# A gated linear attention with an MLP behind it: hand-woven streams against one-engine tasks in a list scheduler's order

## The chip, the core and the metric

The kernel runs on one core of a Trainium2 chip. The metric is the device time of one execution in microseconds (us), as the median of several. The core has five engines that run side by side, each through its own queue and strictly in the order of that queue: TensorE (PE, matrix products and transposes, results to PSUM alone), VectorE (DVE), ScalarE (ACT, exponentials, logs, silu, copies), GpSimd (POOL[...]) and SyncE (SP, which here only starts transfers). They meet through semaphores. So the order in which a kernel emits its instructions is part of its performance: an instruction that is not ready holds all those behind it on its engine.

## The reference: what is computed

Four batches, 8 heads, 768 time steps, head dimension 48. An attention with a forget gate, then an MLP with a silu over all 3072 tokens:

```python
f = 1.0 / (1.0 + np.exp(-f_logit))
for t in range(S):
    state = f[:, :, t, :, None] * state + einsum('bhd,bhe->bhde', k[:, :, t], v[:, :, t])
    y[:, :, t] = einsum('bhd,bhde->bhe', q[:, :, t], state)
x = y.transpose(0, 2, 1, 3).reshape(B * S, H * D)     # 3072 x 384
h = x @ w_in                                          # w_in: 384 x 2048
out = (h * sigmoid(h)) @ w_out                        # w_out: 2048 x 384
```

The kernel works in chunks of 128 time steps. A chunk of all four batches is a *group* g (0 to 5), two of its batches are a *half group*. Within a chunk the loop over time becomes matrix products: the gates' logs are summed along time (`cs`, a product with a triangle of ones), k is multiplied by exp of the sum (`ki`), q by exp of minus the sum (`qg`), both are transposed, their products are masked by the triangle (`atm`), and the output is the masked scores times v plus q times the state before the chunk. The state is then moved on by `d_ps` and the chunk's total decay (`al`).

## The kernel before

Nested Python generators emit the work. Each function below takes one piece of it; most contain steps of several engines in a row (cut to what matters):

```python
def logs(g, lo, hi):                       # ACT, a half or a whole group at once
    f = loaded[g, "f"][:, lo:hi]
    nc.scalar.activation(f, f, AF.Exp, scale=-1.0)
    nc.scalar.activation(lf[g % 3][:, lo:hi, :, 0:D], f, AF.Ln, bias=1.0)

def decays(g, b):                          # PE, then ACT twice
    cs = cps.tile([C, H, D], F32, name="cs", tag="cs")
    nc.tensor.matmul(cs, triu, lf[g % 3][:, b, :, 0:D], start=True, stop=True)
    ...
    nc.scalar.activation(ias[b], cs, AF.Exp, scale=1.0)
    ...
    nc.scalar.activation(aas[b], cs, AF.Exp, scale=-1.0)

def scale_k(g, b):                         # POOL
    nc.gpsimd.tensor_mul(ki[g % 2][:, b, :, 0:D], loaded[g, "k"][:, b], ias[b])
def scale_q(g, b):                         # DVE
    nc.vector.tensor_mul(qg[g % 2][:, b, :, 0:D], loaded[g, "q"][:, b], aas[b])
...
def attend(g, lo, hi):                     # the attention of the units (g, b)
    for s in range(len(units) + 3):
        if s < len(units):
            transposes(g, units[s]);       yield T_COST    # t_ps (PE), qk (DVE)
        if 1 <= s <= len(units):
            scores(g, units[s - 1]);       yield A_COST    # a_ps (PE), atm (DVE)
        if 2 <= s <= len(units) + 1:
            outputs(g, units[s - 2]);      yield Y_COST    # y_ps (PE), y (DVE)
            if g < NCH - 1:
                state(g, units[s - 2]);    yield D_COST    # d_ps (PE), st (DVE)
        if s >= 3:
            turn(g, units[s - 3]);         yield X_COST    # x_ps (PE), xT (DVE)
```

The MLP of a group, in two halves of its work ("in" and "out"):

```python
def mlp_in(g, lo, hi):
    w = (hi - lo) * C                      # 512 columns, or 256 for a half group
    per = MT // w
    for n in range(0, NT, per):
        h_ps = hps.tile([128, per, w], F32, name="h_ps", tag="h_ps")
        for j in range(per):
            for kk in range(KT):           # KT = 3
                nc.tensor.matmul(h_ps[:, j], w_in_sb[:, kk, ...], xT[g][:, kk, lo:hi]..., ...)
        nc.scalar.activation(hT[g][:, n:n + per, lo * C:hi * C], h_ps, AF.Silu)
        yield 650.0

def mlp_out(g, lo, hi):
    for b in range(lo, hi):
        o_ps = hps.tile([C, d_model], F32, name="o_ps", tag="h_ps")
        for n in range(NT):                # NT = 16, a yield after each 4
            nc.tensor.matmul(o_ps, hT[g][:, n, b * C:(b + 1) * C], w_out_sb[:, n, :], ...)
            ...
        nc.scalar.copy(o_sb, o_ps)
        nc.scalar.dma_start(out=out[r0:r0 + C, :], in_=o_sb)
```

PSUM has eight banks, shared out as follows: `cs`/`al_ps` one, `y_ps`/`d_ps`/`x_ps` ("yd") two, `t_ps` one, `a_ps` two, `h_ps`/`o_ps` two. The streams are merged by a rule of proportion (the one with the smallest share of its estimated cost emits next), with leads and splits set by hand:

```python
def interleave_gen(*streams):
    live = [[g, float(total), 0.0] for g, total in streams]
    while live:
        s = min(live, key=lambda s: s[2] / s[1])
        ...
for g in range(1, NCH):
    first = [(mlp_in(g, *span), mlp_cost(*span))]
    ...                                    # with the first 54% of attend(g + 1)
    run(*first)
    second = [(mlp_out(g, *span), mlp_cost(*span))]
    ...                                    # with the rest of attend(g + 1)
        exp_ln_tables()
        logs(g + 2, *ALL)
        lead = 4000.0 if g == 1 else 2000.0
        second.append((chain(wait(lead), prep(g + 2, *ALL, g > 1)), lead + prep_cost(*ALL)))
    run(*second)
```

Group 0 and the beginning of group 1 are written out by hand, with matrix products of zeros (`warm`) in between that keep TensorE's clock up. Inputs arrive by halves for groups 0 and 1 and as whole groups later; after group 0, a tiny transfer (`behind`) that reads a row of `w_out_sb` makes SyncE wait, so that the weights come ahead of group 1.

Of the kernel before, what the change touches and what calls it, by code (L numbers as in the profile page):

```python
# [10 lines left out]
F32 = mybir.dt.float32  # L11
# [6 lines left out]
def interleave_gen(*streams):  # L18


    live = [[g, float(total), 0.0] for g, total in streams]
    while live:
        s = min(live, key=lambda s: s[2] / s[1])
        try:
            s[2] += next(s[0])
            yield
        except StopIteration:
            live.remove(s)


def chain(*gens):
    for gen in gens:
        yield from gen


def once(fn, *args):
    fn(*args)
    yield 330.0
# [3 lines left out]
def kernel(  # L42
# [19 lines left out]
    MT = B * C  # L62

    singles = ctx.enter_context(tc.tile_pool(name="singles", bufs=1))
    ld = ctx.enter_context(tc.tile_pool(name="ld", bufs=2))
    wk = ctx.enter_context(tc.tile_pool(name="wk", bufs=2))
    gk = ctx.enter_context(tc.tile_pool(name="gk", bufs=2))
    hp = ctx.enter_context(tc.tile_pool(name="hp", bufs=2))
    op = ctx.enter_context(tc.tile_pool(name="op", bufs=3))
    cps = ctx.enter_context(tc.tile_pool(name="cps", bufs=1, space=PSUM))  # L70
# [3 lines left out]
    hps = ctx.enter_context(tc.tile_pool(name="hps", bufs=2, space=PSUM))  # L74
# [4 lines left out]
    def load(g, name, b0=0, b1=B):  # L79
        if (g, name) not in loaded:  # L80
            loaded[g, name] = ld.tile([C, B, H, D], F32, name=f"{name}_ld", tag=f"{name}_ld")
        t = loaded[g, name]
        src = SRC[name].rearrange("b h s d -> s (b h) d")[g * C:(g + 1) * C, b0 * H:b1 * H]
        nc.sync.dma_start(out=t[:, b0:b1].rearrange("p b h d -> p (b h) d"), in_=src)

    HB = B // 2
    FIRST, SECOND = (0, HB), (HB, B)
    ALL = (0, B)
    for span in (FIRST, SECOND):
        for name in "fkqv":  # L90
            load(0, name, *span)


    lf = [singles.tile([C, B, H, 64], BF16, name=f"lf{i}") for i in range(3)]
    qg = [singles.tile([C, B, H, 64], BF16, name=f"qg{i}") for i in range(2)]
    ki = [singles.tile([C, B, H, 64], BF16, name=f"ki{i}") for i in range(2)]
    vb = [singles.tile([C, B, H, D], BF16, name=f"vb{i}") for i in range(2)]
# [10 lines left out]
    def load_w_in():  # L108
        src = moe_w_in.rearrange("(ko ki) n -> ki ko n", ki=128)
        for n in range(0, d_ff, 512):  # L110
            nc.gpsimd.dma_start(out=w_in_sb[:, :, n:n + 512], in_=src[:, :, n:n + 512])  # L111
            yield

    def load_w_out():
        src = moe_w_out.rearrange("(ko ki) n -> ki ko n", ki=128)
        for n in range(0, NT, 4):
            nc.gpsimd.dma_start(out=w_out_sb[:, n:n + 4, :], in_=src[:, n:n + 4, :])
            yield

    def exp_ln_tables():  # L120
        nc.scalar.preload_act_table_set("natural_log_exp_and_others")

    alast = {}
    ias = {}
    aas = {}

    def logs(g, lo, hi):

        f = loaded[g, "f"][:, lo:hi]
        nc.scalar.activation(f, f, AF.Exp, scale=-1.0)  # L130
        nc.scalar.activation(lf[g % 3][:, lo:hi, :, 0:D], f, AF.Ln, bias=1.0)  # L131

    def decays(g, b):

        cs = cps.tile([C, H, D], F32, name="cs", tag="cs")
        nc.tensor.matmul(cs, triu, lf[g % 3][:, b, :, 0:D], start=True, stop=True)  # L136
        ias[b] = wk.tile([C, H, D], F32, name="ia", bufs=4)
        nc.scalar.activation(ias[b], cs, AF.Exp, scale=1.0)  # L138
        aas[b] = wk.tile([C, H, D], F32, name="a", bufs=4)
        nc.scalar.activation(aas[b], cs, AF.Exp, scale=-1.0)  # L140

    def scale_k(g, b):
        nc.gpsimd.tensor_mul(ki[g % 2][:, b, :, 0:D], loaded[g, "k"][:, b], ias[b])  # L143

    def scale_q(g, b):
        nc.vector.tensor_mul(qg[g % 2][:, b, :, 0:D], loaded[g, "q"][:, b], aas[b])  # L146

    def scale(g, b):
        scale_k(g, b)
        scale_q(g, b)  # L150
        values(g, b)

    def values(g, b, engine=None):
        src, dst = loaded[g, "v"][:, b], vb[g % 2][:, b]
        if engine is nc.scalar:
            nc.scalar.copy(dst, src)
        else:
            nc.gpsimd.tensor_copy(dst, src)  # L158

    def lasts(g, lo, hi):  # L160
        al_ps = cps.tile([C, B, NP], F32, name="al_ps", tag="cs")
        for b in range(lo, hi):
            for p in range(NP):
                nc.tensor.matmul(al_ps[:, b, p:p + 1], lf[g % 3][:, b, 2 * p:2 * p + 2, :], ones,
                                 start=True, stop=True)
        if g not in alast:
            alast[g] = gk.tile([C, B, NP], F32, name="al")
        nc.scalar.activation(alast[g][:, lo:hi], al_ps[:, lo:hi], AF.Exp, scale=-1.0)

    xT = {}  # L170
    qkT = {}
    atm = {}

    def transposes(g, b):
        i = g % 2
        t_ps = tps.tile([128, 2, NP, C], BF16, name="t_ps")
# [321 lines left out]
```

## Time and profile before

| what | before |
|---|---|
| median of 3 runs | 221.41 us (220.03 to 221.65) |
| profiled run | 220.49 us, span on the core 218.7 us |
| mean granted TensorE clock | 0.961 |
| in tiles: matmuls into h_ps | 192 of 256 columns, 284 ns each as recorded, and 192 of 512 columns, 379 ns |
| out chunks: matmuls into o_ps | 384 of 384 columns, 330 ns |
| silu, one tile of 128x512 | 96 at 597 ns |
| activation table loads | 12 at 1283 ns |
| copy of k scaled (GpSimd) / q scaled (VectorE) | 24 at 1035 ns / 24 at 1012 ns |
| masking of scores (VectorE) | 48 at 686 ns |
| traffic | 25.17 MB read, 4.72 MB written |

How to read it: the span is the time between the first and the last instruction. TensorE's matmuls are pipelined, so the recorded mean of one (330 ns) is longer than the distance between two, and a busy TensorE is not one at its peak. What a row of pieces in the chain of waits gives ("PE o_ps L293 x4", 0.65 us) is nearer to its price. Idle time of an engine that nobody waits for costs nothing; what counts is which wait ends last in a stretch. In the lists, L286 is a line of the kernel, the number before it is the start in us, and the next is how long it took.

### The profile page before, as it was taken

Reading aid. Unit: us, or ns where it says so; the run is one execution under the profiler, and the core shown is the slowest. Engines: PE = TensorE matmul, PEld = TensorE weight load, DVE = VectorE, ACT = ScalarE, POOL = GpSimd, SP = SyncE. Lnnn points to the kernel's source line nnn. Section 1 sums busy time; section 2 is a strip of 40 time slices with the busy share of each in tenths; the row PEclk is TensorE's granted clock in tenths of the full one; section 3 lists DMA queues with packets and bytes.
Section 4 is the critical chain, followed back from the end, with each engine's and each line's share of the span. In section 5 each row is a group of like instructions: output and inputs, shape, how many; then the busy total and the mean of one; then the engine's idle time right before and its main releaser. Section 6 shows DMA issues by size and latency. Waiting matters only on the chain.

```text
span 218.7 us, 4193 instructions
## 1 busy us (share of the span) xinstructions
PE 190.7 (87%) x1740; PEld 117.8 (54%) x1740; DVE 105.3 (48%) x189; ACT 126.2 (58%) x209; POOL 47.7 (22%) x66
## 2 busy tenths in 40 slices
PE   6485899976887687998899998999998999999993
PEld 3244478643675356865455655555654456643561
DVE  3258533126847068787755575456574455200000
ACT  3538267753566555686677846668647760167510
POOL 4317600032320281009200173000462000000000
PEclk9769589999999699999999999999999999999999
DMA  8998999999999999999999962000110000210011
GB/s 138 187 187 111 147 197 181 171 226 197 211 215 165 201 214 214 172 175 221 215 166 198 190 120 76 1 0 3 72 39 36 0 3 36 72 39 0 0 72 72
DMA packets 106034, 27.00 MB, mean 123 GB/s; under 512 B 99360, under 2 KB 106016, under 8 KB 106016
## 3 DMA queue, kind: packets, MB, share of 16 engines
q1 hardware_dynamic: 98848, 18.88, 59.9%
q0 software_dynamic: 3712, 3.15, 9.5%
q10 hardware_dynamic: 3456, 4.72, 6.6%
q8 instruction: 13, 0.21, 0.4%
q14 instruction: 5, 0.04, 0.1%
HBM read 25.17 MB, written 4.72 MB: 137 GB/s over the span
## 4 chain that ended last, share of the span: by engine, by line
PE 60%; DMA 11%; DVE 11%; ACT 9%; POOL 3%; issue 3%; SPq 1%; ACTq 1%; DVEq 0%
PE o_ps L293 22%; PE h_ps L283 22%; DMA w_out_sb<-in_moe_w_out_dram 6%; DVE qg L146 5%; PE t_ps L179 5%; PE a_ps L189 4%; DMA q_ld<-in_q_dram 3%; DMA f_ld<-in_f_logit_dram 2%; DVE qk L181 2%; DVE atm L193 2%; ACT o_sb L298 2%; PE y_ps L211 1%; POOL w_in_sb L111 1%; PE y_ps L215 1%; PE cs L136 1%
## 5 line engine op out<-in xcount | busy, mean ns | idle before, releaser
L283 PE MATMUL h_ps<-xT,w_in_sb 128*128 128x256 bf16 (+1 forms) x384 | 74.6, 332 | 3.7 <-DVE xT L202 1.4
L286 ACT ACTIVATE hT<-h_ps 128x512 bf16<-128x512 f32 x96 | 56.8, 597 | 30.5 <-PE h_ps L283 28.8
L293 PE MATMUL o_ps<-w_out_sb,hT 128*128 128x384 bf16 x384 | 73.0, 330 | 0.1
L283 PEld LDWEIGHTS <-w_in_sb 128*128 128x128 bf16 x384 | 35.1, 99 | 26.2 <-issue 6.0
L293 PEld LDWEIGHTS <-hT 128*128 128x128 bf16 x384 | 35.3, 98 | 25.8 <-issue 6.6
L143 POOL TENSOR_TENSOR ki<-k_ld,ia 128x384 bf16<-128x384 f32 x24 | 24.8, 1035 | 110.8 <-ACT ia L138 110.8
L193 DVE TENSOR_TENSOR atm<-a_ps,triu 128x512 bf16<-128x512 f32 x48 | 30.9, 686 | 17.5 <-PE a_ps L189 17.5
L146 DVE TENSOR_TENSOR qg<-q_ld,a 128x384 bf16<-128x384 f32 x24 | 23.7, 1012 | 21.1 <-ACT a L140 14.9
L298 ACT COPY o_sb<-o_ps 128x384 f32<-128x384 f32 x24 | 11.5, 477 | 25.4 <-PE o_ps L293 25.0
L181 DVE COPY qk<-t_ps 128x1024 bf16<-128x1024 bf16 x24 | 16.6, 690 | 17.7 <-PE t_ps L179 17.7
L241 DVE TENSOR_TENSOR st<-d_ps,al 48x192 bf16<-48x192 f32 x40 | 14.2, 354 | 17.6 <-PE d_ps L237 17.2
L138 ACT ACTIVATE ia<-cs 128x384 f32<-128x384 f32 x24 | 11.8, 490 | 17.7 <-PE cs L136 15.3
L158 POOL CAST vb<-v_ld 128x384 bf16<-128x384 f32 x22 | 15.3, 699 | 6.0 <-DMA v_ld<-in_v_dram 6.0
L130 ACT ACTIVATE f_ld<-f_ld 128x768 f32<-128x768 f32 (+1 forms) x8 | 9.3, 1163 | 11.0 <-DMA f_ld<-in_f_logit_dram 11.0
L136 PE MATMUL cs<-lf,triu 128*128 128x384 bf16 x24 | 8.2, 342 | 8.0 <-ACT lf L131 4.3
L179 PE MATMUL t_ps<-ident,qg 128*128 128x128 bf16 x96 | 9.8, 227 | 5.4 <-DVE qk L181 3.6
L202 DVE CAST y<-y_ps 128x384 bf16<-128x384 f32 x22 | 12.2, 553 | 4.2 <-PE y_ps L215 4.0
L179 PEld LDWEIGHTS <-qg 128*128 128x128 bf16 x96 | 7.5, 100 | 10.8 <-issue 5.4
L189 PE MATMUL a_ps<-qk 48*128 48x128 bf16 x192 | 10.2, 229 | 2.6 <-DVE atm L193 2.6
L189 PEld LDWEIGHTS <-qk 48*128 48x128 bf16 x192 | 5.8, 98 | 11.0 <-issue 7.2
L140 ACT ACTIVATE a<-cs 128x384 f32<-128x384 f32 x24 | 11.7, 486 | 0.0
L215 PE MATMUL y_ps<-vb,atm 128*128 128x48 bf16 x192 | 11.4, 185 | 0.0
(40 smaller groups left out, 145.7 us busy)
## 6 DMA issues: line engine op xcount, KB each, us to landing
out_dram<-o_sb ACTq DMA_DIRECT2D x24, 192.0 KB, 2.1
f_ld<-in_f_logit_dram SPq DMA_DIRECT2D x4, 768.0 KB, 10.3
k_ld<-in_k_dram SPq DMA_DIRECT2D x4, 768.0 KB, 11.1
q_ld<-in_q_dram SPq DMA_DIRECT2D x4, 768.0 KB, 11.1
v_ld<-in_v_dram SPq DMA_DIRECT2D x4, 768.0 KB, 11.4
f_ld<-in_f_logit_dram SPq DMA_DIRECT2D x4, 384.0 KB, 5.4
k_ld<-in_k_dram SPq DMA_DIRECT2D x4, 384.0 KB, 6.2
q_ld<-in_q_dram SPq DMA_DIRECT2D x4, 384.0 KB, 6.6
```

The lines of the kernel that those rows point to most:

```text
L143: nc.gpsimd.tensor_mul(ki[g % 2][:, b, :, 0:D], loaded[g, "k"][:, b], ias[b])
L146: nc.vector.tensor_mul(qg[g % 2][:, b, :, 0:D], loaded[g, "q"][:, b], aas[b])
L158: nc.gpsimd.tensor_copy(dst, src)
L179: nc.tensor.transpose(t_ps[:, j, p, :], src[i][:, b, 2 * p:2 * p + 2, :], ident)
L181: nc.vector.tensor_copy(sb, t_ps)
L189: nc.tensor.matmul(a_ps[:, r, p, :], qkT[b][lo:lo + D, 1, p, :], qkT[b][lo:lo + D, 0, p, :], start=True, stop=True)
L193: nc.vector.tensor_mul(sb[:, r], a_ps[:, r], triu[:, None, :].to_broadcast([C, NP, C]))
L241: nc.vector.tensor_mul(st[b][lo:lo + D, :, r * D:(r + 1) * D], d_ps[lo:lo + D, :, r * D:(r + 1) * D], alast[g][lo:lo + D, b, :, None].to_b ...
L283: nc.tensor.matmul(h_ps[:, j], w_in_sb[:, kk, (n + j) * 128:(n + j + 1) * 128], xT[g][:, kk, lo:hi].rearrange("p b c -> p (b c)"), start=( ...
L286: nc.scalar.activation(hT[g][:, n:n + per, lo * C:hi * C], h_ps, AF.Silu)
L293: nc.tensor.matmul(o_ps, hT[g][:, n, b * C:(b + 1) * C], w_out_sb[:, n, :], start=(n == 0), stop=(n == NT - 1))
L298: nc.scalar.copy(o_sb, o_ps)
```

## The change

The generators are gone. The work is described as tasks, each on one engine, with an estimated duration, the tasks it needs, the buffer that it takes and those it frees, the activation table it uses, and a rank. A list scheduler in Python runs over them while the kernel is being built, always taking the task that can start first (of several that can, on one engine, the one of lowest rank), and the instructions are emitted in the order of its start times. The MLP tasks have ranks above 1000, so on TensorE attention goes first and the MLP fills what is left. "In" and "out" tasks follow modes, so that ScalarE need not swap its tables at each silu; the filler of zeros is put into planned gaps until the first MLP task. What it is for: no engine's queue should have a task at its head that waits while one behind it is ready.

Beside the order, these things change:

- everything goes by half groups (12 of them): loads (four buffers of half groups in place of two of whole ones), logs, the MLP (always 256 columns, two blocks to a tile);
- `cs` and `al_ps` go into the two "yd" banks, and `h_ps`/`o_ps` get a third bank;
- `behind` reads row 4 of `w_out_sb` (second quarter of the weight) in place of row 10 (third quarter), and all weights are issued in one go;
- the copies out of PSUM that ScalarE made at the start (y and xT of the first units) are VectorE's.

The core of the diff (cut; the removed code is that above):

```diff
+class Plan:
+    DRAIN = {"PE": 0.19, "DMA": 2.0}
+    TABLE = 1.28
...
+            for e, cands in fronts.items():
+                cands = [c for c in cands if self.allowed(c, fronts, free)]
...
+                first = min(s for s, _, _ in cands)
+                now = [c for c in cands if c[0] <= first + 1e-6]
+                choice = min(now, key=lambda c: c[2]["rank"])
+                if best is None or choice[0] < best[0]:
+                    best = choice
...
+    def allowed(self, cand, fronts, free):
+        start, swap, t = cand
+        kind = t["name"][0]
+        if kind in "IO" and t["engine"] == "PE":
+            if kind == self.mode:
+                return True
+            now = [c for c in fronts.get("PE", ()) if c[2]["name"][0] == self.mode and c[0] <= start + 0.7]
+            pending = self.mode == "I" and self.silus
+            return not now and not pending and not (kind == "I" and self.exps)
...
-    ld = ctx.enter_context(tc.tile_pool(name="ld", bufs=2))
+    ld = ctx.enter_context(tc.tile_pool(name="ld", bufs=4))
-    cps = ctx.enter_context(tc.tile_pool(name="cps", bufs=1, space=PSUM))
-    hps = ctx.enter_context(tc.tile_pool(name="hps", bufs=2, space=PSUM))
+    hps = ctx.enter_context(tc.tile_pool(name="hps", bufs=3, space=PSUM))
...
+    def cumsum(m, j):
+        cs[m, j] = yps.tile([C, H, D], F32, name="cs", tag="yd")
+        nc.tensor.matmul(cs[m, j], triu, lf[m % 4][:, j, :, 0:D], start=True, stop=True)
...
+    def mlp_in(m, n):
+        h_ps = hps.tile([128, 2, HT], F32, name="h_ps", tag="h_ps")
+        for i in range(2):
+            for kk in range(KT):
+                nc.tensor.matmul(h_ps[:, i], w_in_sb[:, kk, (n + i) * 128:(n + i + 1) * 128],
+                                 xT[m][:, kk].rearrange("p b c -> p (b c)"),
+                                 start=(kk == 0), stop=(kk == KT - 1))
+        hs[m, n] = h_ps
...
+    plan = Plan({"yd": 2, "t": 1, "a": 1, "h": 3, "qk": 3, "atm": 2, "y": 2, "ia": 4, "aa": 4,
+                 "hT": 4, "xT": 4})
...
+            add(n("cs"), "PE", 0.165, do(cumsum, m, j), [f"L{m}"], rank=r, takes="yd", opens=1)
+            add(n("ia"), "ACT", 0.4, do(inverse, m, j), [n("cs")], rank=r, table="exp", takes="ia")
+            add(n("aa"), "ACT", 0.4, do(forward, m, j), [n("cs"), n("ia")], rank=r + 1, table="exp", takes="aa", frees=[n("cs")], opens=-1)
...
+            add(n("T"), "PE", 0.45, do(transposes, m, j), [n("qg"), n("ki")], rank=r + 5, takes="t")
+            add(n("qk"), "DVE", 0.65, do(transposed, m, j), [n("T")], rank=r + 4, takes="qk", frees=[n("T")])
...
+            add(f"I{m}.{n}", "PE", 0.655, do(mlp_in, m, n),
+                [U("xT", m, j) for j in range(HB)] + [f"wi{n // 4 * 512}"] + ([f"I{m}.{n - 2}"] if n else []),
+                rank=1000 + m * 10 + n * 0.1, takes="h", frees=[U("xT", m, 0)] if n == NT - 2 else None)
+            add(f"S{m}.{n}", "ACT", 0.64, do(silu, m, n), [f"I{m}.{n}"], rank=-1000 + m, table="silu",
+                frees=[f"I{m}.{n}"], takes="hT" if n == 0 else None)
...
+        nc.sync.dma_start(out=behind, in_=w_out_sb[0:1, 4, 0:64])
+    add("weights", "POOL", 6.5, weights, [U("ki", 1, 1)], rank=-10)
...
+        plan.run(warm, "I0.0")
+        plan.emit()
```

## The prediction

> **What bounds the kernel now.** I read the page's totals first, then a table of the span cut at places where the kind of work changes, then the chain that ended last inside the two places that look wrong. The cuts are mine: 24.0 is the first matrix product of the MLP, 59.26 the first of the second group of 128 time steps (h_ps for group 1), 84.32 the start of a dense stretch, 134.58 roughly the end of input traffic, 215.0 the last copy out of PSUM.
>
> ```profile
> PE 190.7 (87%) x1740; PEld 117.8 (54%) x1740; DVE 105.3 (48%) x189; ACT 126.2 (58%) x209; POOL 47.7 (22%) x66
> ```
>
> ```profile
> core 0: us, PE busy (x) PEld busy (x) DVE busy (x) ACT busy (x) POOL busy (x), PEclk, DMA share, GB/s
> 0.00:24.00 24.00, 15.19 (x126) 8.62 (x126) 12.64 (x23) 12.04 (x21) 11.97 (x24) 0.81 1.10 151
> 24.00:59.26 35.26, 30.56 (x299) 21.79 (x300) 14.97 (x32) 19.68 (x36) 5.86 (x9) 0.94 1.22 195
> 59.26:84.32 25.06, 19.16 (x194) 13.46 (x194) 13.25 (x21) 16.56 (x25) 9.06 (x11) 0.93 1.32 202
> 84.32:134.58 50.26, 47.24 (x501) 30.31 (x499) 34.78 (x63) 33.22 (x53) 13.67 (x16) 1.00 1.14 175
> 134.58:215.00 80.42, 78.51 (x624) 43.59 (x623) 29.68 (x52) 44.18 (x75) 7.13 (x9) 1.00 0.09 30
> ```
>
> TensorE is the only engine near the span, and everywhere but in the first 84 us it is busy nearly all the time. The third and fourth rows are the hole: 60 us of which TensorE was busy 50, with a granted clock below 1. So the question is what TensorE had to do in each stretch and what it took.
>
> Unit prices, all from pieces of the chain of waits at full clock: 6 matmuls of 256 columns into h_ps (one "in" tile) 0.66 us; 4 matmuls into o_ps (one "out" chunk) 0.65; per (half group, batch) unit of attention t_ps 0.45, a_ps 0.35, y_ps 0.38, d_ps 0.33, x_ps 0.2, cs 0.16, and 0.08 as its share of al_ps: 1.95 in all. The MLP of a half group is 8 tiles and 8 chunks, 10.5 us; with its two units of attention 14.4.
>
> In 134.58 to 215.0 the kernel does 48 tiles and 48 chunks (62.9 us), attention of two groups less the work of the last state and already made sums (13.3): 76.2 of 80.4, a loss of 4.2. In 84.32 to 134.58 it is 47 tiles and chunks (30.8) and about 14.7 of attention: 45.5 of 50.3, loss 4.8. In 59.26 to 84.32 it is 10 tiles, 8 chunks (11.8) and some 4 of attention: about 16 of 25, loss 9. In 24 to 59.26 it is 32 tiles and chunks of group 0 (21) and about 6.5 of attention, loss 7 to 8. The two last losses are what a new order can win; the dense stretches hold 9 more.
>
> What makes the loss in the third stretch is seen in the chain of waits:
>
> ```profile
> 68.03 0.60 ACT hT L286
> 68.63 0.02 issue
> 68.65 1.28 ACT L121
> 69.93 0.01 issue
> 69.94 1.49 ACT f_ld L130
> 71.43 0.02 issue
> 71.46 1.49 ACT lf L131
> 72.95 0.04 issue
> 72.99 0.48 PE cs L136
> 73.47 2.57 PE o_ps L293 x8
> ...
> 79.67 3.14 DVE qg L146 x4
> ```
>
> The sum cs of group 2 stands at the head of TensorE's queue and waits for a table load (1.28) and two whole-group logs (1.49 each), while ready out chunks stand behind it; TensorE idles 2.6 us, its clock drops, and the next 8 matmuls take 2.57 instead of 1.30. Then four scalings of q in a row (3.14) hold the transposes. This is wrong order, not missing capacity.
>
> What makes a dense stretch lose is seen near the end, where nothing but in tiles runs:
>
> ```profile
> 193.94 1.46 PE h_ps L283 x6
> 195.40 0.04 issue
> 195.43 1.46 PE h_ps L283 x6
> ```
>
> Two tiles (6 matmuls of 512 columns here) each 1.50 us. The same 6 matmuls elsewhere in the chain take 1.29. The silu is 0.597 us: with two banks a bank's cycle is matmul 0.65, silu 0.61, and two handovers, 1.50 for two tiles, 0.75 each in place of 0.65.
>
> **What the Trainium skill says.** "PSUM — Partial Sum Buffer", Summary: rules for kernel authors, says to evacuate promptly since PSUM is tight; and "Perfetto Trace Analysis", Optimization Strategy, says that the same gap repeating on the engine that should be saturated can mean too few buffers for the next tile. The 1.50 us beat agrees. "TensorE: Matmul & The Clock Gate", What's actually happening, says the array starts at half rate and falls back to it after an idle window of about 3.4 us; here about 2.6 us idle went before the half-speed matmuls at 73.5, so the trace agrees in kind. "ScalarE: Activation LUTs", What ACT_TABLE_LOAD costs, gives 1283 ns for a load plus some 1380 ns of drain; the trace has 1283 ns for each of 12, but the silu begins at once after it (69.93 to 69.94 for the log): no drain of that size is seen.
>
> **The change, part by part.**
>
> *Third MLP bank.* The sums cs and al_ps move to the two "yd" banks, and their bank goes to h_ps/o_ps. On 14 to 16 bare tiles at the end that is 0.75 to 0.66, 1.3 us. Where tiles alternate with attention the gain is partial, and the three banks let TensorE run 2 us ahead while ScalarE loads a table (before, it stood from about 60.7 to 61.16 for that). I put 2 to 3 us on the whole, half of the loss in the dense stretches.
>
> *One column width.* All in tiles are now two blocks of 256 columns, so 576 matmuls in place of 384. 6 of 256 take 0.66, 3 of 512 take 0.645: 48 tiles by 0.015 is 0.7 us more, and weight loads stay hidden (98 ns against a pitch of 110).
>
> *Start, to 24 us.* The eight input loads are the same bytes in the same order; the first in tile waits for the first quarter of w_in, whose issue now stands behind four ki and two vb on GpSimd. By the old durations the fourth ki ends near 18.2 us, against an issue at 18.46 before. More filler matmuls keep the clock up, but w_in (a chunk each 2.4 us) sets the pace to 31. Gain about zero to 1.
>
> *24 us to the first h_ps of the third half group (before: 59.26).* The w_in chunks arrive to about 30.4, then 8 tiles at 0.66 against 0.75: the out chunks start near 37 instead of 38.9. The guard transfer that lets input loads resume now waits for the second instead of the third chunk of w_out, 2.4 us sooner, but those loads then share the engines with the rest of w_out: f of group 1 lands about 41 instead of 42.3. In the built order cs stands behind 12 out chunks (to 45), then ia 0.49, a 0.4, qg 1.0, t_ps, qk 0.7, a_ps, atm 1.3, y_ps, y 0.55, x_ps, xT. The DVE queue has both qg ahead of the first qk, and the second exponential stands behind a result copy and al, so I add: a 46.4, second a 47.8, second qg 48.8, qk 49.5, first atm 51.4, second atm 55.3, y and xT 56.8. Few out chunks are left by then, and TensorE idles here about 5 us and may lose its clock for 1 to 2. First h_ps: 56.5 instead of 59.26, and without the 0.5 us table stop.
>
> *The rest.* From that point: 80 tiles by 0.655 and 80 chunks by 0.65 are 104.4; attention of nine half groups: 18 units by 1.38 (t, a, y, x) 24.8, 14 d by 0.33 4.6, 16 sums 3.8, together 33.2. Sum 137.6. Before, the two dense stretches paid 9.0 on 121.7, that is 7.4%. With the third bank and single-engine tasks I take 4%: 5.5. The holes of 59 to 84 do not come back as such: logs are per half group (0.84 twice), out chunks stand ahead of cs in the built order, and only two qg come in a row.
>
> *Sum.* 56.5 + 137.6 + 5.5 is 199.6 for the last out chunk, the tail (copy, issue, landing) stays at 3.7: span 203.3. The reported time of the profiled run is 1.8 above its span (220.49 against 218.7), the median another 0.9: 205 to 206.
>
> **Rivals.** *First: ScalarE becomes the bound through tables and order.* The built order has 14 table loads in place of 12 (2.6 us more), and ScalarE would carry about 140 us in some 205. Against: 68%, and in the bare tile stretches its 0.63 per tile is below TensorE's 0.655. For: single queue, in order; an exponential behind a silu that waits on TensorE, which waits for the exponential's consumer, would ripple. If it costs another 6 us: 212.
>
> *Second: the two yd banks.* cs, al, y, d and x now share two banks, and cs holds one until both exponentials are done. In the built order both cs of a half group are often issued just before a run of 7 or 8 in tiles, so both banks stay taken through it. The order keeps y, d and x away from those runs, but any lateness of ScalarE stalls TensorE directly. Speaks for it: cs waited for a (3.7 us in all) already with a bank of its own. 3 to 8 us: 209 to 214.
>
> *Third: the transfers set the pace.* A half group's loads are 8.3 us at the 190 GB/s of the busy slices, and TensorE needs 14.4 for it; four buffers of half groups hold as much as before. After 57 us this cannot bind. Only the wait for group 1 stays, which is counted.
>
> *Fourth: the schedule fits its estimates and not the chip*, so that one late task holds a queue whose other tasks are ready. Its durations stand close to the trace (silu 0.64 against 0.60, qk 0.65 against 0.69, atm 1.25 against 1.29, exponentials 0.4 against 0.39 to 0.49; k and q scalings 1.0 and 0.95 against 1.035 and 1.012, though with single ones from 0.54 to 1.7). I expect small slips. If they were everywhere, the loss per half group would be 2 us and the time 218.
>
> **Range and chances.** 206, with the first h_ps at 54.5 to 58 and losses of 2 to 12 after it: 200 to 213. Faster by 2% means under 217.0, which needs 11 us of the 15 to go wrong: 0.88 for faster, 0.08 for the same, 0.04 slower.
>
> **What would show it.** h_ps of the third half group near 56.5; no idle of 2.6 us in front of cs with out chunks ready; bare tiles at 0.66 each at the end; table loads 14; TensorE busy over 93% from 57 us on; granted clock 1 after 60. It is wrong if waits for yd banks (y, d, x or cs for ScalarE's a) sum to more than 5 us, if ScalarE's table loads stand in the chain again and again, or if the first third slips by more than 3 us.

## The result, and the profile after

The changed kernel takes 212.33 us in the median of four executions (212.27 to 214.04), against 220.72 us for the kernel before on the same chip. The ratio is 0.9639, with a 95% interval of 0.9569 to 0.971: faster by 3.6%. The prediction was 206.0 with a range of 200 to 213. The direction and the range hold, the range near its upper end; the gain is 8.4 us instead of about 15.

The page's totals of the changed kernel, and the row of the granted clock (a digit for each 5.26 us):

```profile
PE 191.8 (91%) x1957; PEld 140.6 (67%) x1957; DVE 99.7 (47%) x198; ACT 127.0 (60%) x220; POOL 45.9 (22%) x66
...
PEclk9999769999958999999999999999999999999999
```

TensorE is as busy as before (191.8 against 190.7 us), in a span of 210.5 instead of 218.7: what went is idle time. The clock falls twice; by single microseconds, it is at half from 23 to 30 us and from 57 to 64.

The span cut at the same kinds of places as before: 24.43 is the first in tile, 39.24 the first out chunk, 59.64 the first h_ps of the third half group, 206.77 the end of the last out chunk (columns as in the prediction's table: length, busy time of PE, PEld, DVE, ACT, POOL with counts, granted clock, DMA share, GB/s).

```profile
39.24:59.64 20.40, 16.88 (x158) 10.51 (x156) 8.63 (x17) 11.90 (x22) 6.34 (x8) 0.95 1.15 214
59.64:75.08 15.44, 15.44 (x148) 11.51 (x148) 7.85 (x16) 9.22 (x13) 0.96 (x2) 0.85 1.25 186
75.08:92.43 17.35, 13.11 (x156) 10.43 (x155) 8.39 (x16) 13.50 (x23) 4.26 (x6) 1.00 1.23 203
...
127.07:206.77 79.70, 79.67 (x822) 59.33 (x819) 35.59 (x66) 46.41 (x85) 10.31 (x11) 1.00 0.17 48
```

From 127 us on TensorE has no idle time left (79.67 of 79.70), where the kernel before was busy 78.51 of 80.42 and, beyond that, waited inside pairs of tiles. The hole of 59 to 84 us has become a row of 15.44 without idle time but at a clock of 0.85, and a row of 17.35 that is busy 13.11. And the first half is late: out chunks begin at 39.24 and the third half group at 59.64, no earlier than before (59.26).

The end, in the chain of waits of the changed kernel:

```profile
181.97 9.17 PE h_ps L353 x84
191.14 15.61 PE o_ps L368 x96
```

84 matmuls are 14 in tiles: 0.655 us each, where the kernel before took 1.50 for two. The beat is gone.

**Three places where time is lost.** The first is in front of the third half group (start, duration, what; the chain of waits):

```profile
45.15 7.68 DMA k_ld<-in_k_dram
...
52.91 0.34 ACTq L376
...
53.29 0.85 ACT f_ld L231
...
55.06 0.34 PE cs L238
```

L376 starts the transfer of a finished output tile, from ScalarE's queue. The copy it sends was done at 51.29, but the issue goes out only at 52.91, the moment a load of k for a later half group has landed. ScalarE has no use for that k. Behind the issue, in the same queue, stand the exponential and the log of half group 3 (f_ld and lf); the sum cs waits for those, and everything to 59.64 follows from cs. There is little slack beside it, though: y_ps, which follows cs at 57.17, also needs a masking (atm) that VectorE ended only at 56.59. So without this wait y_ps could have come at most about 0.6 us earlier here. In the built program this output transfer and that load of k count on the same completion semaphore: there are eight, handed out in turn to loads and outputs alike, so the second must wait for the first to land before it is issued.

The second is among in tiles, further on in the same chain:

```profile
87.46 1.28 ACT L224
...
88.75 0.85 ACT f_ld L231
...
89.63 0.84 ACT lf L232
...
90.49 1.28 ACT L224
...
92.43 3.44 PE h_ps L353 x30
```

ScalarE leaves its silus, loads the table for exponential and log (1.28), does one half group's logs (1.69), and loads the silu table again (1.28). Three banks are full after 1.97 us of in tiles, and TensorE stands for 2.7. It is the longest of TensorE's waits in the changed kernel (total, times, longest):

```profile
PE h_ps L353 <- ACT hT L362: 2.7, 1, 2.7
```

The third is the half clock at 57 to 64: 12 matmuls of the third half group take 2.72 us from 59.64, against 1.31 at full clock. A smaller fourth is at 75 to 78, where the log of half group 5 stands ahead of the exponentials of half group 4 on ScalarE, and TensorE idles 1.4 us (0.63 and 0.78).

### The profile page after: what moved, and what is told of

Same layout as the page of the kernel before. It is cut to its first block, busy times and chain, and to the rows that moved or that the text cites. A ratio compares the mean times of both kernels' runs of the same rounds, so it can differ in the third digit from the quotient of the medians.

```text
span 210.5 us, 4687 instructions
## 1 busy us (share of the span) xinstructions
PE 191.8 (91%) x1957; PEld 140.6 (67%) x1957; DVE 99.7 (47%) x198; ACT 127.0 (60%) x220; POOL 45.9 (22%) x66
## 4 chain that ended last, share of the span: by engine, by line
PE 66%; DMA 12%; ACT 7%; SPq 4%; DVE 4%; POOL 3%; issue 2%; ACTq 0%; DVEq 0%
PE h_ps L353 24%; PE o_ps L368 22%; DMA w_out_sb<-in_moe_w_out_dram 6%; PE t_ps L278 4%; PE w_ps L381 4%; SPq L192 4%; DMA k_ld<-in_k_dram 4%; DMA q_ld<-in_q_dram 3%; PE a_ps L290 3%; PE y_ps L306 2%; PE y_ps L310 2%; ACT f_ld L231 2%; POOL w_in_sb L213 2%; PE cs L238 1%; ACT L224 1%
## 5 line engine op out<-in xcount | busy, mean ns | idle before, releaser
L353 PE MATMUL h_ps<-xT,w_in_sb 128*128 128x256 bf16 x576 | 73.0, 282 | 5.8 <-ACT hT L362 2.7
L368 PE MATMUL o_ps<-w_out_sb,hT 128*128 128x384 bf16 x384 | 67.8, 326 | 0.0
L353 PEld LDWEIGHTS <-w_in_sb 128*128 128x128 bf16 x576 | 56.1, 101 | 15.1 <-issue 4.2
L254 DVE TENSOR_TENSOR qg<-q_ld,a 128x384 bf16<-128x384 f32 x24 | 19.3, 814 | 55.6 <-ACT a L248 55.5
L317 DVE CAST y<-y_ps 128x384 bf16<-128x384 f32 x24 | 13.4, 556 | 12.2 <-PE y_ps L310 11.9
L257 POOL CAST vb<-v_ld 128x384 bf16<-128x384 f32 x22 | 12.1, 576 | 24.3 <-DMA v_ld<-in_v_dram 12.3
L231 ACT ACTIVATE f_ld<-f_ld 128x768 f32<-128x768 f32 x12 | 10.1, 843 | 8.2 <-DMA f_ld<-in_f_logit_dram 6.2
L381 PE MATMUL w_ps<-zeros 128*128 128x384 bf16 x53 | 12.4, 386 | 1.1 <-DVE zeros L483 1.1
L310 PEld LDWEIGHTS <-atm 128*128 128x128 bf16 x192 | 10.0, 98 | 4.1 <-DVE atm L297 2.1
L306 PE MATMUL y_ps<-st,qk 128*128 128x96 bf16 x80 | 9.9, 204 | 1.1 <-DVE xT L328 0.7
```

Source lines behind the costliest of these rows:

```text
L254: nc.vector.tensor_mul(qg[m % 4][:, j, :, 0:D], loaded[m, "q"][:, j], aas[m, j])
L310: nc.tensor.matmul(y_ps[:, 2 * p + r, :], atm[m, j][:, r, p, :], vb[m % 4][:, j, 2 * p + r, :], start=not opened, stop=True, skip_group_ch ...
L353: nc.tensor.matmul(h_ps[:, i], w_in_sb[:, kk, (n + i) * 128:(n + i + 1) * 128], xT[m][:, kk].rearrange("p b c -> p (b c)"), start=(kk == 0 ...
L368: nc.tensor.matmul(os[m, j], hT[m][:, i, j * C:(j + 1) * C], w_out_sb[:, i, :], start=(i == 0), stop=(i == NT - 1))
L381: nc.tensor.matmul(w_ps[:, 0:NP * 2 * D], zeros[:, 0:128], zeros, start=True, stop=True)
```

## The experiments

My theory A: the order and the third bank work as meant; what is missing from the gain is the three places above (tables, half clock, the output issue). Rivals: the order gains little and the third bank does the work, or the reverse; and, for each place, that its time comes back as another wait. Every ratio is of means, against runs of the kernel before in the same batch, and leaves out executions over 1.5% above the fastest of the same kernel, which is why a median (of all) and a ratio can differ (in e9 these are three of six). Intervals are 95%. Those of e1, e4 and e5 overlap that of the changed kernel a little, though each of their executions was shorter than each of its four; so "2 us less" is rough there, and what an edit did is read from its trace.

| run | what it is | us, median | ratio (interval) |
|---|---|---|---|
| after | | 212.33 | 0.9639 (0.9569 to 0.971) |
| e1 | no table exchange among in tiles | 210.38 | 0.9537 (0.9488 to 0.9586) |
| e2 | scheduled order, banks of before | 209.37 | 0.9489 (0.9451 to 0.9526) |
| e3 | old order, new banks | 220.19 | 0.996 (0.9928 to 0.9991) |
| e4 | zeros that keep the clock | 210.78 | 0.9546 (0.949 to 0.9601) |
| e5 | one output issued by GpSimd | 210.45 | 0.9554 (0.9485 to 0.9624) |
| e6 | log of half group 5 later | 212.49 | 0.9644 (0.959 to 0.9697) |
| e7 | e1, e4, e5, e6 together | 207.89 | 0.9439 (0.9392 to 0.9487) |
| e8 | e2 with e4 and e5 | 211.77 | 0.9585 (0.9531 to 0.9638) |
| e9 | ten outputs issued by GpSimd | 211.8 | 0.9505 (0.9439 to 0.957) |
| e10 | e9 with e1 and fewer zeros than e4 | 206.22 | 0.9359 (0.9316 to 0.9402) |
| e11 | e2 with e9 | 207.85 | 0.9432 (0.9381 to 0.9483) |

### e1: no table exchange among in tiles

```diff
-        if t["table"] == "exp" and not t["opens"] and self.mode == "I" and self.silus:
+        if t["table"] == "exp" and not t["opens"] and self.mode == "I":
```

> The changed kernel, but no task that needs the exponential table may be planned while the in tiles are running (in the changed kernel the log of half group 6 is put between the silus of half groups 3 and 4, with a table load on each side, at 87.5 to 91.8 us, and TensorE waits 2.65 us for silu at 92.4). Table loads 12 instead of 14; TensorE's order is the same up to that place. Theory A (that swap is a term of its own that the prediction left out): the wait of h_ps for hT of 2.65 us is gone and the time is 2 to 3 us lower, about 209.5 to 210. Rival (ScalarE has its work to do anyway, and the log comes later where it hurts as much, by holding cs): the time stays within 1 us of the changed kernel's 212.3.

It took 210.38 us, 2 less than the changed kernel, and has 12 table loads instead of 14. The in tiles of the disputed stretch now run through (chain of waits of this run):

```profile
86.99 5.24 PE h_ps L353 x48
```

The exchange was worth about what it stood for, 2.0 of 2.65 us; from the first h_ps of the third half group to the last out chunk this run takes 145.0 us, where the changed kernel takes 147.1.

### e2: the scheduled order with the old banks

```diff
-    hps = ctx.enter_context(tc.tile_pool(name="hps", bufs=3, space=PSUM))
+    cps = ctx.enter_context(tc.tile_pool(name="cps", bufs=1, space=PSUM))
+    hps = ctx.enter_context(tc.tile_pool(name="hps", bufs=2, space=PSUM))
...                                        # cs and al_ps back into cps; the planner is told
-    plan = Plan({"yd": 2, "t": 1, "a": 1, "h": 3, ...
+    plan = Plan({"yd": 2, "t": 1, "a": 1, "h": 2, "cs": 1, ...
```

> The list scheduler with the old banks: h_ps/o_ps two, cs and al_ps one of their own, and the scheduler is told so. Theory A (the third bank is worth the 1.50 against 1.31 us for two bare tiles, some 14 bare tiles at the end and part of the other 82): 2 to 4 us slower than the changed kernel, 214 to 216, and the two-tile beat of 1.50 is back near the end. Rival (the order is everything and the two yd banks cost what the third bank gives): within 1 us of the changed kernel, or faster.

A miss: it took 209.37 us and beats the changed kernel. The beat of two banks is there at the end, as expected (chain of waits of this run):

```profile
185.33 1.47 PE h_ps L354 x12
...
186.83 1.47 PE h_ps L354 x12
```

But the plan is a different one. With another resource to obey the planner happened to make 10 table loads in place of 14, and no exchange among in tiles; its third half group began at 57.63 instead of 59.64. So this run does not price the bank alone: here a list scheduler turned one changed resource into another order.

### e3: the old order with the new banks

The kernel before, with its h_ps in three banks and cs and al_ps in the two yd banks, as in the change; nothing else.

> The kernel before with its own order, only the banks changed: cs and al_ps go into the two yd banks, h_ps/o_ps get three. Theory A: the beat of 1.50 us for two bare tiles at the end becomes 1.31 (1.3 to 1.5 us there), but the waits at 71 to 73 and 79 to 83 us stay, and cs now waits for y, d and x too: 1 to 3 us faster than the kernel before, about 218 to 219.5. Rival (banks are most of the gain): 5 us or more faster, 215 or below.

220.19 us, ratio 0.996: without the new order the bank is worth 0.4%, about 0.9 us (0.2 by the medians). The beat at the end is cured (46 matmuls in one run), and the waits in front of cs stay (first the chain of waits of this run, then TensorE's waits):

```profile
191.96 10.09 PE h_ps L282 x46
```

```profile
PE cs L135 <- ACT lf L130: 4.5, 2, 2.6
```

That is the old wait for whole-group logs, 2.6 us at its longest, as in the kernel before. Logs by half groups came together with the new order, and no run has the one without the other.

### e4: zeros that keep the clock

Matrix products of zeros (which nobody reads) in the places where TensorE waits in the first 60 us: 14 ahead of the first in tile, 4 ahead of that of the third half group, 15 around the attention of half groups 2 and 3.

```diff
+        if n == 0 and m in (0, 2):
+            warm(14 if m == 0 else 4)
```

> The changed kernel with matmuls of zeros added in the two places where TensorE waits and then runs at half clock: 14 ahead of the first in tile (it waits 2.5 us for w_in at 22 to 24.4), and 19 in six small groups between y_ps of the third half group and its first in tile (50 to 59.6). Nothing else moves. Theory A (half clock costs about 2 us at 24 to 31 and about 2 us at 59.6 to 63): granted clock 1 there, 6 matmuls of an in tile take 0.66 and not 1.3, the first in tile of half group 2 starts 0 to 2 us earlier than 59.6 and the time is 2 to 4 us lower, 208.5 to 210.5. Rival (w_in's transfers set the pace to 31 us, and the later stretch is set by VectorE's chain, so a faster TensorE only waits more): within 1 us of the changed kernel.

210.78 us, 1.5 less: smaller than expected. The clock was 1.00 from 24 to 90 us, and still the third half group began at 59.31: ScalarE's wait at the output issue sets that, whatever the clock. The wait for the silu after the exchange remained, and after it the clock fell there instead (0.83 from 90 to 100).

### e5: one output issued by GpSimd

```diff
-        nc.scalar.dma_start(out=out[r0:r0 + C, :], in_=o_sb)
+        queue = nc.gpsimd if (m, j) == (1, 1) else nc.scalar
+        queue.dma_start(out=out[r0:r0 + C, :], in_=o_sb)
```

> The changed kernel with one output transfer, the fourth (half group 1, second batch), issued from GpSimd's queue in place of ScalarE's. ScalarE's and TensorE's other instructions keep their order. In the changed kernel ScalarE finishes the copy for it at 51.29 us but issues it at 52.91, because that transfer counts on the same completion semaphore as the load of k for half group 3, which lands at 52.9; the log of half group 3 stands behind it, then cs of half group 3, and behind that, on TensorE, the last attention of half group 2. In the runs with other starts ScalarE stood there for 4.2 us (no swap) and 3.0 us (kept warm), and the first in tile of half group 2 began at 59.3 in all of them. Theory B (the shared semaphore sets that time): ScalarE takes the log when f has landed, near 50 to 51.5, and the first in tile starts 1.5 to 3 us earlier, 56.5 to 58; time 1 to 2.5 us lower than the changed kernel's 212.3, 210 to 211.3. Rival (VectorE's chain of qg, qk, atm, y, st, xT, or f itself, sets it): the first in tile stays within 0.7 us of 59.3, time within 1 us.

210.45 us, 1.9 less. ScalarE's wait for k is gone; the log of half group 3 waits for f itself, which it does need, and starts at 50.76 instead of 53.29; the third half group begins at 57.42 instead of 59.64. The four executions differ: spans of 207.2 (twice, mean clock 0.991) and 210.1 and 210.3 (0.968). Three of the changed kernel's do not: 210.5 and 210.6 at a clock of 0.968, 210.5 at 0.984 (the fourth is 212.3 at 0.959). The two causes lie side by side, as the 0.6 us of slack in front of y_ps said. While ScalarE stands at the issue, a slow clock ahead of the first out chunks costs little; once it does not, the clock's fall at 23 us would show, and these 3 us are most likely that (the longer executions have no trace).

### e6: the log of half group 5 after the exponentials of half group 4

```diff
-    def logs(m):
+    def logs(m, late=False):
+        if m == 5 and not late:
+            return
...
+        if (m, j) == (4, 1):               # after the second exponential of half group 4
+            logs(5, True)
```

> The changed kernel with one thing moved on ScalarE: the two log instructions of half group 5 stand after the exponentials of half group 4, and not between that half group's log and its exponentials. All other engines keep their order. In the changed kernel cs of half group 4 is ready at 74.2 us, but its first exponential starts at 76.0, after 1.7 us of the other log and a result copy, and TensorE has no out chunk left from 76.3 to 78.05. Theory C (the scheduler takes a task that can start now over one on the critical chain that can start 0.35 us later): the exponential starts near 74.4, TensorE's idle time of about 2 us between 75 and 78 shrinks to under 0.7, time 1 to 1.7 us lower, 210.6 to 211.3. Rival (the log is needed soon anyway, cs of half group 5 then comes late): time within 0.7 us.

212.49 us: no gain. The first of these exponentials moved from 76.01 to 75.12, less than expected, and the log came out between them and the silu table (chain of waits of this run):

```profile
79.12 0.84 ACT lf L234
...
79.98 1.28 ACT L224
...
81.92 0.81 PE h_ps L357 x6
```

The in tile at 81.92 waited 1.29 us for that silu, and t_ps before it 0.57 for qg: 1.9 us in place of 1.4. The rival is right in that the time moved to the next place, which is the silu and not cs. This loss stays uncured here.

### e7 and e8: the mendings together

> All four edits in one: no table swap between in tiles, kept warm (10 zeros in place of 14 ahead of the first in tile), the fourth output on GpSimd's queue, the log of half group 5 after the exponentials of half group 4. If the four losses are separate and lie one after another on TensorE's path, the gains add: 2 (measured) + 1.5 (measured) + 1.5 to 2.5 + 1 to 1.7, so 204.5 to 206.5 us. If they share the same slack, or a stall only moves to the next place, it stays at 208 or above.

> The list scheduler with the old two banks for the MLP (209.4 us), kept warm and with the fourth output on GpSimd's queue. It has 10 table loads and no swap among its in tiles. Theory: 1 to 1.5 from the clock and 1 to 2 from the semaphore: 206 to 207.5. If it comes out at or below the mended kernel with three banks, the third bank has no worth under this scheduler.

Both miss. e7 (with 10 zeros ahead of the first in tile instead of 14) took 207.89 us, ahead of each single mending but short of their sum, and e8 (10 zeros there too) took 211.77, more than e2 without the mendings. In both, another output than the one that was moved waits for a load. In e7 it is the third output (ScalarE's instructions in order of time), whose copy ends at 47.48 and whose issue goes at 49.10:

```profile
46.98 0.50 ACT L390 COPY o_sb<-o_ps 128x384 f32<-128x384 f32 x1
49.10 0.34 ACTq L393 DMA_DIRECT2D out_dram<-o_sb  x1
```

That output shares its semaphore with the load of v of half group 2, in the changed kernel as in e7. There its copy ends at 49.09 and the issue follows at 49.12; here the copy is earlier, and meets the load: the cast of that v on GpSimd, which waits for it too, starts at 49.08. (Which transfer has which semaphore is again read from the built programs.) Two more things hold e7's third half group to 60.40: its first q lands only at 47.5, and the zeros are not free. They stand in TensorE's order, and two groups of them came ahead of pieces that were ready (1.28 us at 52.72, where the masking for y_ps ended at 53.09, and 0.49 at 55.77); together this is about 1 us, by my estimate from these ends.

In e8 it is an output at 89, in the midst of the dense part (in brackets the idle time ahead, and what ended it; the trace is of one of the longer executions, 213.56 us):

```profile
89.54 0.49 ACT L246 ACTIVATE ia<-cs 128x384 f32<-128x384 f32 x1 [2.64 <-DMA k_ld<-in_k_dram]
```

Here the semaphores did change. There are eight in turn, and with one output moved out of the round, later transfers get others: in e2 this output follows another output on its semaphore and is issued at once (copy to 86.54, issue at 86.56), in e8 it follows a load of k.

That asked for a cure that leaves no output among the loads' semaphores while loads run.

### e9, e10, e11: the first ten outputs issued by GpSimd

```diff
-        nc.scalar.dma_start(out=out[r0:r0 + C, :], in_=o_sb)
+        queue = nc.gpsimd if m < 10 else nc.scalar
+        queue.dma_start(out=out[r0:r0 + C, :], in_=o_sb)
```

(`m` counts half groups: ten of the twelve, two tiles each, so 20 transfers. The texts below call them ten tiles.) e9 is the changed kernel with this alone; e10 has the edit of e1 and some zeros besides (8 ahead of the first in tile, not 14); e11 is e2 with this.

> The changed kernel with one difference: the output transfers of the first ten tiles are issued by GpSimd instead of ScalarE (the transfers themselves, and every order of TensorE, are the same). Theory (ScalarE stands at output issues because an output counts on a semaphore that a load still in flight also counts on): no ScalarE instruction waits for a load it does not read, first hidden matmul of the third half group at 57 to 58 instead of 59.64, and the exchange of tables among the in tiles stays; 209.5 to 211.0 us, as the run that moved one output alone (210.45). Rival (it is only the one collision of the third half group, and a moved output makes GpSimd, which is in order, stand for the copies and hold its casts of k and v): no better than 211.5.

> The changed kernel with three differences: the rule against the exchange of tables, a few warming matmuls of zeros before waits in the first 60 us, and the first ten output transfers on GpSimd. In the run with all four mendings (207.89) ScalarE stood at the third output's issue instead of the fourth's. Theory: with no output on ScalarE there is no such place left, first hidden matmul of the third half group at 57 to 58 instead of 60.4, no gap over 1 us on TensorE from there to the end; 205.5 to 207.3 us. Rival (GpSimd now stands for the copies, and its casts come late, or the time saved at the third half group goes into the next wait for a load): 207.5 or more.

> The scheduled order with the banks of the kernel before (two for the hidden layer, one for cs) and the first ten output transfers on GpSimd; nothing else. Theory: as with three banks ScalarE loses its stands at output issues (up to 2.6 us in the run with two banks, one output moved and warming): 207.0 to 209.0 us, against 209.37 with the outputs on ScalarE; first hidden matmul of the third half group at 56.5 to 57.6. Rival (two banks make the MLP wait for ScalarE's silus at every stretch, so what is gained ahead is lost behind): 209 to 211.

ScalarE's waits in e9, the part on transfers:

```profile
ACT f_ld L231 <- DMA f_ld<-in_f_logit_dram: 7.6, 3, 3.6
...
ACT vb L260 <- DMA v_ld<-in_v_dram: 2.4, 1, 2.4
```

Only loads that it reads are left. The third half group begins at 57.70. GpSimd does stand for the copies, 61.3 us in 13 waits, as the rival had it, but ScalarE and TensorE do not visibly pay for it: GpSimd is 27% busy. The time does not decide between the two: the ratio of 0.9505 is 209.5 us on the 220.43 of its batch, at the edge of the theory's 209.5 to 211.0, while the median of all six, 211.8, is on the rival's side of 211.5. What decides is the trace. Its executions again fall apart by clock: spans of 206.9 and 208.9 at 0.983, and 211.1 to 211.3 at 0.96.

e10 joins it to the edit of e1 and to the zeros, and took 206.22 us, 0.9359, in the middle of the 205.5 to 207.3 expected: the fastest of all, and its interval lies wholly under that of the changed kernel. Its totals and its clock:

```profile
PE 191.4 (94%) x1982; PEld 139.6 (68%) x1982; DVE 104.9 (51%) x198; ACT 124.0 (61%) x218; POOL 56.7 (28%) x86
...
PEclk9999999999999999999999999999999999999999
```

Out chunks begin at 37.10, the third half group at 58.02, the clock is full throughout. One gap over 1 us is left after that (t_ps at 74.28 waits 1.22 for qg), which I had said would not be there.

e11 took 207.85 us, 0.9432, also as the theory had it: 1.5 under e2, with intervals that overlap. Between e10 and e11 lies the third bank in two plans that have neither exchange nor output wait: 1.6 us. Their intervals just overlap (0.9381 to 0.9402), and the plans differ in more than the bank (10 table loads in e11, 12 in e10), so that figure is rough.

## Why the prediction was right, and where its size was off

**The mechanism.** "Wrong order, not missing capacity" holds as far as the banks go. The banks without the order gave 0.4% (e3); everything but the banks gave 5.1% (e2). That everything is more than an order, though: half-group logs and loads, one column width and the earlier guard transfer are in it, and no run takes them apart. The 2.6 us in front of cs with ready out chunks behind it is gone, and so is the 1.50 us beat.

**Third bank, "2 to 3 us".** Too large. It is 0.9 us in the old order (e3) and about 1.6 in the new (e10 against e11). The term of 1.3 us for 14 bare tiles at the end was right (0.655 a tile); what I added for alternating stretches is not there, presumably since attention's own pieces there already give ScalarE the time to empty a bank (not shown).

**One column width, 0.7 us.** Right in its price: 0.655 a tile of 256 columns, with no idle time between.

**Start and first out chunk, "near 37".** 39.24 in the profiled execution. The first issue of w_in came at 19.20, where the prediction had the last ki end at 18.2; TensorE stood 2.5 us for it, and its clock fell for nearly 7 us. In the other scheduled runs, whose clock held there, the out chunks began at 36.1 to 37.9. Mended alone this error would have brought little: e1 began them at 36.1 and its third half group still at 59.27.

**First h_ps of the third half group, "56.5".** This is the step that failed: 59.64, outside the 54.5 to 58 given for it. (The walk itself ends at xT, 56.8, which is later than 56.5.) It followed that half group's own chain, and the real path did not run there alone. The second masking, "55.3", ended at 56.59, with the out chunks 2.2 us late. From there to xT was to be 1.5 us and took 3.0. On TensorE the cs of half group 3 came before y_ps, and y_ps waited for the exponentials of that sum (first VectorE, then TensorE):

```profile
55.30 1.29 DVE L297 TENSOR_TENSOR atm<-a_ps,triu 128x512 bf16<-128x512 f32 x2
```

```profile
57.17 0.20 PE L306 MATMUL y_ps<-st,qk 128*128 128x96 bf16 x1 [0.43 <-ACT a L248]
```

That sum was late because an output issue, to which the prediction gave no wait, stood for a load that ScalarE does not read; and the half clock stretched the last pieces. With the outputs elsewhere the third half group begins at 57.0 to 58.0 (e5, e9, e10, e11), within about 1.5 us of the 56.5, with out chunks at 36.7 to 37.9. Both errors were gone there; e5's longer executions, only 0.2 to 0.4 us under the changed kernel's 210.5, suggest that the hold alone was worth little too.

**The rest, 137.6 us of need and 5.5 of losses.** From 59.64 to 206.77 are 147.1 us, so losses were 9.5. They are: the exchange 2.65, half clock at 59.6 to 64.4 2.3 (a clock of 0.85 over 15.44), idle time at 75 to 78 1.4, idle time from 92 to 127 0.7; some 2 us are spread and I can't name them. I had counted the two extra table loads as a rival (212) and not in the sum. The need itself fits: in e10, from 58.0 to the end of the last out chunk at 201.2 are 143.2 us, a loss of 5.6 against the 5.5 predicted. That it comes so near is partly luck, since the 5.5 was taken for a kernel with the exchange in it. On the other side, the 0.9 us that the prediction added between profiled run and median did not come (212.27 and 212.33).

**The tail, 3.7 us:** 3.73.

**The rivals.** The first (ScalarE through tables and order) is what happened in part: 14 loads, one exchange that TensorE waited for, and 212. That the time is its 212 is chance: it put 6 us on this, and e1 returns 2. ScalarE's load was 127.0 us, 60%, and not about 140. The second (two yd banks) did not: the waits for ScalarE's a, for st and for xT in front of cs, al_ps and y_ps are 3.9 us in seven, none over 0.8, against the 5 us that I had named as the mark. The third (transfers) I set aside "after 57 us", and by volume it does not bind. It did before that, through a semaphore and not through bytes. The fourth is small: where slips show, they are one place each.

**What would show it.** Table loads 14: yes. TensorE over 93% busy from 57 on: 144.0 of 149.8, 96%. Clock 1 after 60: no, half clock to 64. No idle 2.6 us in front of cs with out chunks ready: yes. One of the signs of being wrong came true: the first third slipped by 3.1 us, where 3 was the mark.

Put together: of the 6.3 us between 212.3 and 206.0, e10 returns 6.1 with three edits that leave the order's principle alone. How much is each one's can't be added up, since they lie partly side by side (e5, e7).

## What to carry to other kernels

A scheduler is as good as the dependences it is told of. Here it knew data, buffers and tables, but not that a transfer's issue waits for an earlier transfer on the same completion semaphore; keep such issues off the queue of an engine that is on the critical path (e9 to e11), or give them semaphores of their own (not tried). Filler that keeps a clock up stands in the queue too, and can hold what is ready (e7). When a change makes a planner run again, compare plans by what they contain (table loads, runs of tiles, waits) before calling the difference the effect of the edit. And when two causes of delay lie side by side, mend both in one run before judging either.

## What the runs showed of the hardware that was not expected

**An output waits for a load.** A transfer out of ScalarE's queue was held 1.6 us (after), 4.2 (e1), 1.6 (e7) and so long that ScalarE idled 2.6 (e8), each time until a load on SyncE's queue landed. The Trainium skill, "DMA: Bandwidth & Descriptors", Why a DMA increments its semaphore by 16 and not by 1, says that two transfers in flight on one semaphore can't be told apart by its count, and asks for one semaphore per slot in flight. I take the hold to be the price of sharing safely. That it is the shared semaphore I read from the built program; the runs show that it ends with the load's landing, and goes when the issue moves to GpSimd (e5, e9). I did not run a version with more semaphores on ScalarE's queue.

**The clock falls without a long idle time.** TensorE's clock in the changed kernel, by single microseconds:

```profile
22.00:23.00 1.00, 0.00 (x0) 1.00 1.17 178
23.00:24.00 1.00, 0.00 (x0) 0.65 1.14 174
...
54.00:55.00 1.00, 0.64 (x11) 1.00 1.06 265
55.00:56.00 1.00, 0.58 (x2) 1.00 1.28 255
56.00:57.00 1.00, 0.34 (x8) 1.00 0.91 153
57.00:58.00 1.00, 0.83 (x15) 0.72 1.34 227
58.00:59.00 1.00, 0.94 (x8) 0.50 1.29 181
...
63.00:64.00 1.00, 1.00 (x8) 0.50 1.38 187
```

Behind the length stands TensorE's busy time with its count, then the granted clock. A mean of 0.65 over the microsecond from 23 is a fall from 1 to half at about 23.3, and 0.72 over that from 57 one at about 57.4. "TensorE: Matmul & The Clock Gate", What's actually happening, gives an idle window of about 3.4 us. The first fall came some 1.3 us into a wait of 2.5. Ahead of the second no idle time from 50 on is longer than 0.8 us; TensorE was busy 0.64, 0.58 and 0.34 in the three microseconds from 54 to 57, and the clock then stayed at half for over 6 us, four of them fully busy. So a gap shorter than that window is not safe here, and with zeros in these places (e4) the clock was 1.00 from 24 to 90 us. But the fall is not certain either: e9 and e5 had the same wait of 2.5 us at 22 and kept full clock. What decides it no run here shows. The microsecond from 23 in e9:

```profile
23.00:24.00 1.00, 0.00 (x0) 1.00 1.06 149
```
